# Two attention-and-MLP layers on one core: query ratio on GpSimd, parked sums joined by VectorE, a last step in open banks, and a new order

## The chip, the cores and the metric

The kernel runs on one core of one Trainium2 chip. The metric is device time in microseconds, from the first to the last instruction of an execution and a little around it; the time before is the median of three runs.

Five engines have queues of their own. TensorE (PE) multiplies, VectorE (DVE), ScalarE (ACT) and GpSimd (POOL) do elementwise work, and SyncE (SP) issues all data transfers. Results of PE land in eight PSUM banks of 512 float32 columns each.

## The reference

```python
def _A_ref(x, wqkv, w_phi, wo):          # S = 2048 rows, D = 512, H = 32 heads of 16
    q, k, v = split(x @ wqkv)
    pq, pk = q @ w_phi, k @ w_phi        # per head
    phi_q = concat([softmax(pq), softmax(-pq)])
    phi_k = concat([softmax(pk), softmax(-pk)])
    kv = einsum("bhsf,bhsd->bhfd", phi_k, v)     # sums over all rows
    z  = einsum("bhsf->bhf", phi_k)
    num = einsum("bhqf,bhfd->bhqd", phi_q, kv)
    den = einsum("bhqf,bhf->bhq", phi_q, z)[..., None] + 1e-6
    return (num / den) @ wo

def _B_ref(x, w1, w2):                   # hidden width 1792
    return maximum(x @ w1, 0) @ w2

x = x + _A_ref(layernorm(x), ...)
x = x + _B_ref(layernorm(x), ...)
x = x + _A_ref(layernorm(x), ...)        # the same weights once more
x = x + _B_ref(layernorm(x), ...)
```

## The kernel before

Each float32 product is made of three float16 products (high by high, high by low, low by high: `PAIRS`). The 2048 rows are 16 chunks of 128 (`NCH`), and two chunks make one of the eight tiles of the MLP (`NT`).

**A layer.** Every chunk is normalised (`front_norm`), its keys and values are projected (`keys`, `values`), and `gather` adds the products of key features and values to the running sums. The sums of 16 pairs of heads are spread over three groups (`SPANS`: 7, 7 and 2 pairs, 66 columns each). When all 16 chunks are in, `summary` folds the two 33-column halves of each pair together and makes the right-hand side of the numerators. Each chunk's query goes through `query` and `look`; `numerators`, `turn` and `back_project` finish the attention; then come the MLP's tiles in seven steps each (`tile_steps`).

**Products by seven.** Most MLP tiles compute a 2x2 block product with seven products instead of eight. `hidden_by_seven` issues those of the first weight in one PSUM bank `ph`: ACT saves parts of the bank (`snap`, L1484), DVE adds a saved part in the middle of each step (`plus`, L1490) and two at its end (`both`, L1495), and PE goes on after those. `out_by_seven` does the same for the second weight, in four banks (y0, y1, kv1, kv0) that stay open over the steps of a tile; `leave` takes the four banks out into the two row blocks `xa` and `xb` with ACT, DVE and POOL. The last step of the last tile is computed plainly: `mlp_out` for the first chunk and `last_rows`, in two halves, for the second, in banks of their own, each with its own DVE addition to the rows (L1602, L1622).

**Parked sums.** In layer 0's last tiles the next layer's sums are gathered already, while the banks kv0 and kv1 are wanted by `out_by_seven`. So after chunk 9 ACT copies the sums aside (`save`, L896), chunks 10 and 11 are made in another bank and added by DVE (`added`, L887), and at chunk 12 the sums are put back into banks by multiplying them with the identity on PE (`back`, L873).

**The query features.** `feature_map` with `psum=False` computes, per chunk, two softmaxes over 16 columns: DVE takes the sums and the ratio of the two (`ratios`, L728 to L730), ACT raises one half and makes a guard (L734, L738), POOL multiplies the other half by the ratio (`product`, L747), ACT rounds (L757), POOL makes the low part (L761), and SP turns the result into `pT`.

**The order.** Each task of the kernel names its engine, its reads and its writes; the task's number beside it is the planner's estimate of its duration. `ORDER` holds one long string per engine, in which each character says which of the tasks still left on that engine comes next. The five queues are thus written out by hand; waits between engines follow from the reads and writes.

Of the kernel before, what the change touches and what calls it, by code (L numbers as in the profile page):

```python
# [9 lines left out]
F32 = mybir.dt.float32  # L10
# [8 lines left out]
P = 128  # L19
# [6 lines left out]
LAG = 2  # L26
# [6 lines left out]
ASIDE = 2 * (NT - 3)  # L33
# [25 lines left out]
        "000033220100220031000010000a190840055051391301538473008402a0302920a302100105206020612031F051C4B20z133140"  # L59
        "3140304770663gg00ee10cccc0bbbb0iaagafae00170605500302011900110000010045030004061110001215020033040045000"  # L60
        "78008809a00101156360541022110600020000000600700000000000000000000050700d00bh000j000000g00000000000000000"
        "0011111333333330222444444133022233344440022222222000000000111220000033007c000000080000000002000002200000"
        "0000000201111100000200300000000000000070900f000c0hm000000j000j0000000000e0000000000000011111111111333333"
        "33302233341330222222222222222233344444440355044445555566677788888aaa099900770600446666660044400222222222"
        "22011111100000000000000000001111110110000111000011111444440302222255555555044444488077777066605999999999"
        "9990880020000050090000090000000000000001111111110010p0oq012l0l1jj000hgg000fddddi00b10dff0ccccc00aaa09900"
        "770004444407383366304031105005040000022010001105504444555aaaaaaaaaaaaaaaaaaabbbccccccccdddeee00200999000"
        "6620033330222011111111100500600000000h00i00000000000f00000000l0000L00000J0000000V0000000000O00000R000000"
        "000000000000000000H00000000000000X00000000000000000J000000000000000000000000E00F00000000000C000000000000"
        "000000000000000p000000000000000000000000000000p00000000000h00000000s000s0000000000000000000h000000000000"  # L70
        "0i0L000L0000000000U00000000000000000000D000000000000000000000q0000000000u0000000000000000000000000000000"
        "00000000000000000000000000000000000000000000000000000000000000000000000000000000000000000000000000000000"
        "000000000000000000000000000000000000000000000000000000000000000010",
    DVE:
        "330343302321000f51441192412111601c0b33j0503584c730g2230c000e0YYd0g00eS044e4Ndg66Jie0500440a302h20f1h11f0"
        "0g00i0d7063c5b55c04a44033300111441026051002m32k2k3j22g22222b2233232282335i2340e2d211116191lt127i52n2fl30"
        "0112018f12d9940002660779bb0891aa0781c0b1520362001bb141070013131152131216310361756715073056050a402001411c"
        "3b222843120123350242000011111133443022504030a0181062e2d0101900001313115213121150416886716910706625000801"
        "601000111136306216552407363343514030999g0ff002d201091000006320314047312161241103001025223003602401060500"
        "8001650067555402844002201066014007732200h4g0001221180000005704003010000000373024010000000k01i00h0f0000b0"  # L80
        "a01001b1a403700030g20e10cx2w01511101030tl232p255mMM24090HO0N70Zd7Zc76I0Z8285804123a491201Z2Z201ZxZ06Zvb1"
        "01j30Zoi3042Zt10Zr21h11fZl000ZOZO112cc01100ZE1190m1315j013101101k1ZtZtj0231005232200220Zc062521072252102"
        "2e2002b21020200243228800220770b25o21062501h0220022102hh3060042320b0290170a292800221020102010202005223200"
        "2200201020102000220023000233201022002210221020000010011010",
    ACT:
        "00424312110044010002005cbbb5a02me9kd808260dm310j2902dl2kc1040uZq30kk3213mmZhZg02Zep722m5sll20o306ll62113"
        "61l2k4L212420kk421011023g01e1400301cc0131gg21131gg21131050102d3k42046212c12108lll80b0hh6c9e090f478664080"
        "2050bb009014d1039111c1054483203029i909006c14bee0a004688a000b20b90a8001669013404340605c505413674034534303"
        "62240063001c1600033101410041201206811645b444441320510133001556000434001103734305223228230042472104b41483"
        "025530222223601102024088b21009480b30010001211217460565042232721055a59088848477c01ab0ade0eii0d10e2420f008"  # L90
        "00668071905775533a39933393577303a23820732102016670085102403214130011400442008188b33101004100103730322204"
        "05040064301100050440j301g11821304016004090d8c80b0aa6a07500c4602202103030241310d03889a008058506n066l55i60"
        "60e5o8347kl06I0Hh90F840B6P76Zq6M687K7ZjI66Zh7b070043Z8Zo440ZY220Zi4Zi4r41Zd33ZL440ZJ0010ZVs33ZB3024442ZK"
        "2ZZm24ZI401114102200302200504x23015400228100Z75247163ZA00Zzm120041033204002Zi01Zw10220105040302404312Zc1"
        "16052406024420006410322501L307250130200502330s60130262005j04416304427030604e0204102200302620143022614002"
        "620055040605203005104032500302500302040022003020103022040302000303201030220002221400221030200000",
    POOL:
        "10002540850058006800960A70y8016810960060908a000790070a1180900700020106252201b010837b205500550010e10c0i0h"
        "00bj0i09b18d0c700d52035103009080560500020550700570104523221111403000113020100304443300112313101100101112"
        "1504009240353403212111400002013101114104443301034300010010bb0a010777090555556601433302002011022201110000"  # L100
        "0050030000000030010000011100330000066605000000000a091000200b009cc0kk0uY29s0U8110Z00110Vj1Zm20Zk11m0Zp003"
        "302222g201Zc111ZB1111000070n01100100201121330211d11040310111T1411Y152202113302203302141101008222u2225000"
        "0504131102d2201330211d1211122017000070010330005222002221100044403333333333331000000000022201110000000000",
    SP:
        "30200110102600169d30520bx6c47c40rce6g16545d03401x9331dy1ac2111007k24h20g1123q131001b606gld02f20u2is03231"
        "34273Af5732de22eb11ec141441a99n129524b139339383b7982769b749488a66214g0307b36375a2df567426e3a90826i554007"
        "36272pb76777468694a947k7264f4284748c2f2g21e3410a121d14992308d82bb7ba275100447036502702n2ma419773745t1t31"
        "23p160p5t06061000E3030z12a02630h720pd010rl1170uaa60B097e20h3B0a1Jdd20Nbe5Vjbcea0baj2T484p7Z04ea44q98d038"
        "252552P130200i04053607240441b2260511706329203201191505036026424330015511551441302203022200010",
# [173 lines left out]
def tile_kernel(ctx: ExitStack, tc: tile.TileContext, x_in, wqkv, w_phi, wo, w1, w2, out):  # L283
# [17 lines left out]
            "rhs0": 1, "rhs1": 1, "r46": 2, "s46": 5, "s46a": 4, "yT": 2, "oT": 2, "h0": LAG + 3, "h1": LAG + 3, "w2": 3, "sn": 2}  # L301
# [360 lines left out]
    def feature_map(src, inv, up, side, psum, fast, name, pool=fr, tags=("e", "p16")):  # L662
# [17 lines left out]
        for h in range(0, H, n):  # L680
# [45 lines left out]
            def ratios(of=piece_of):  # L726
                sm, e3 = of()[2], of()[5]
                nc.vector.tensor_reduce(sm, e3, axis=AX.X, op=ALU.add)  # L728
                nc.vector.reciprocal(sm[:, H:], sm[:, H:])
                nc.vector.scalar_tensor_tensor(sm[:, H:], sm[:, :H], HALF, sm[:, H:], op0=ALU.mult, op1=ALU.mult)  # L730
# [128 lines left out]
    def gather(l, c):  # L859
# [6 lines left out]
        parted, again = ASIDE <= c < ASIDE + CPT, c == ASIDE + CPT  # L866
        if c == 0 or again:
            kv_bank[l] = [bank(f"kv{i}", f"kv{i}_{l}_{c}") for i in range(2)]
        if again:
            def back():  # L870
                for i, (b, a) in enumerate(zip(kv_bank[l], aside)):
                    b.ap = b.make()
                    nc.tensor.matmul(of_pairs(b.ap, i), ident, of_pairs(a.ap, i), start=True, stop=False,  # L873
                                     skip_group_check=True)

            add(PE, 1.56, back, reads=aside, makes=kv_bank[l])
        if not parted:
            sums_of_pairs(l, c, range(2), kv_bank[l], c == 0, c in (NCH - 1, ASIDE - 1))
        for i in range(3) if parted else (2,):
            b, a = bank("n", f"kvn{i}_{c}"), rest if i == 2 else aside[i]  # L880
            sums_of_pairs(l, c, [i], {i: b}, True, True)

# [1242 lines left out]
```

## Time and profile before

| what | value |
|---|---|
| median of three runs | 963.53 us |
| lowest of them | 962.7 us |
| profiled execution | 964.9 us |
| its span | 962.8 us |
| granted TensorE clock, mean | 0.999 |
| instructions | 23735 |

The profile is of one execution. Its page gives each engine's busy time, the span in 40 slices, the chain of work that ended last, the costliest groups of instructions, and the transfers. Other views group instructions by line, list who waited for whom, or show a stretch in order of time. PE is TensorE's products and PEld its weight loads, which overlap them; a "q" behind an engine's name is its sequencer, and SPq issues transfers. In a group's row stand the line, the engine, the operation, output<-input, the count, and behind the bar the busy time in us and the mean of one in ns. In a row of one line's view stand minimum, median and maximum in ns. In a timeline row stand start and duration in us, and in brackets the idle time before it with what ended it.

### The profile page before, as it was taken

How to read it: one execution, taken by the hardware profiler on the slowest of the kernel's cores; microseconds unless marked ns; L12 is line 12 of the kernel's file. 1: busy time of each engine (PE TensorE's matmuls, PEld its weight loads, DVE VectorE, ACT ScalarE, POOL GpSimd, SP SyncE). 2: the span in 40 equal slices, each digit the busy share in tenths (PEclk: the TensorE clock that was granted, in tenths of full speed). 3: DMA queues.
4: the chain of work that ended last, by engine and by line, in shares of the span. 5: the costliest groups of instructions: out<-in, count | busy, mean ns of one | idle time of the engine just before them, and what ended most of it. 6: DMA issues, size and time to landing. Idle time of an engine off the chain costs nothing.

```text
span 962.8 us, 23735 instructions
## 1 busy us (share of the span) xinstructions
PE 948.0 (98%) x9368; PEld 658.8 (68%) x9368; DVE 708.2 (74%) x1445; ACT 588.2 (61%) x1161; POOL 618.8 (64%) x634
## 2 busy tenths in 40 slices
PE   8999999999999999999999999999999999999997
PEld 6544455665665666667677875566666989888997
DVE  6999988876977778676476678887887566655554
ACT  8999888754564646455365555566556566555553
POOL 2697865758874757655277646256377887777563
PEclk9999999999999999999999999999999999999999
DMA  8657459469689696968739765579899776956441
GB/s 309 211 160 219 132 145 240 92 144 211 176 216 256 170 219 180 238 176 213 194 122 271 254 203 155 169 189 262 202 225 238 217 176 152 219 135 187 141 136 64
DMA packets 251839, 183.38 MB, mean 190 GB/s; under 512 B 180688, under 2 KB 188112, under 8 KB 251728
## 3 DMA queue, kind: packets, MB, share of 16 engines
q1 hardware_dynamic: 251728, 181.87, 72.1%
q8 instruction: 73, 1.20, 0.6%
q14 instruction: 38, 0.31, 0.1%
HBM read 108.30 MB, written 30.15 MB: 144 GB/s over the span
## 4 chain that ended last, share of the span: by engine, by line
PE 85%; DVE 5%; DMA 5%; ACT 2%; POOL 2%; issue 1%; SPq 0%; DVEq 0%; POOLq 0%; ACTq 0%
PE ph L1471 22%; PE py L1587 13%; PE py L1646 12%; PE pk L653 8%; PE pv L653 8%; PE pq L653 8%; PE pw L653 7%; PE ph L1551 3%; DMA oT<-n_o 2%; PE pn L1056 2%; PE kv L852 1%; DMA s<-s_dram 1%; DMA st_k<-in_A_wqkv_dram 1%; DVE fm_q L728 0%; POOL n_o L570 0%
## 5 line engine op out<-in xcount | busy, mean ns | idle before, releaser
L1587 PE MATMUL py<-w,h 128*128 128x512 f16 x690 | 174.5, 379 | 0.0
L1484 ACT ACTIVATE sn<-ph 128x128 f32<-128x128 f32 x294 | 80.7, 274 | 151.2 <-PE ph L1471 147.6
L1471 PEld LDWEIGHTS <-s 128*128 128x128 f16 x2352 | 151.2, 98 | 27.1 <-issue 3.1
L653 PEld LDWEIGHTS <-xT 128*128 128x128 f16 x900 | 86.8, 98 | 98.2 <-issue 1.7
L1471 PEld LDWEIGHTS <-w 128*128 128x128 f16 x1764 | 111.0, 98 | 13.8 <-DVE h L1202 0.6
L1471 PE MATMUL ph<-yT,s 128*128 128x128 f16 x1176 | 97.6, 219 | 2.5 <-DVE ph L1490 2.4
L1471 PE MATMUL ph<-yT,w 128*128 128x128 f16 x1176 | 97.6, 219 | 0.0
L1587 PEld LDWEIGHTS <-h 128*128 128x128 f16 x690 | 61.3, 98 | 47.4
L1490 DVE TENSOR_TENSOR ph<-ph,sn 128x128 f32<-128x128 f32 x98 | 29.3, 299 | 87.0 <-PE ph L1471 50.3
L761 POOL TENSOR_TENSOR p_q<-e_q,p_q 128x1024 f16<-128x1024 f32 x32 | 72.3, 2260 | 24.8 <-ACT p_q L757 24.7
L653 PE MATMUL pw<-wo_h,oT 128*128 128x512 f16 x256 | 81.2, 379 | 2.1 <-DMA oT<-n_o 1.9
L750 POOL TENSOR_TENSOR e_k<-e_k,fm_k 128x1024 f32<-128x1024 f32 x30 | 58.4, 1948 | 36.3 <-ACT fm_k L742 31.1
L653 PE MATMUL pv<-wv_h,xT 128*128 128x512 f16 x256 | 81.5, 379 | 0.0
L653 PE MATMUL pk<-wk_h,xT 128*128 128x512 f16 x256 | 81.5, 379 | 0.0
L761 POOL TENSOR_TENSOR p_k<-e_k,p_k 128x1024 f16<-128x1024 f32 x30 | 67.2, 2241 | 21.7 <-ACT p_k L757 19.8
L653 PEld LDWEIGHTS <-oT 128*128 128x128 f16 x384 | 36.7, 98 | 44.4 <-DMA oT<-n_o 4.1
L1646 PEld LDWEIGHTS <-h 128*128 128x128 f16 x648 | 59.2, 98 | 7.3 <-issue 0.7
L1495 DVE TENSOR_TENSOR ph<-ph,sn 128x256 f32<-128x256 f32 x98 | 41.9, 427 | 28.7 <-PE ph L1471 27.8
L747 POOL TENSOR_TENSOR e_q<-e_q,fm_q 128x512 f32<-128x512 f32 x32 | 33.9, 1060 | 41.2 <-DVE dn L1064 17.7
L1267 POOL TENSOR_TENSOR w<-r 128x256 f32<-128x256 f32 x41 | 32.7, 797 | 40.5 <-ACT r L1263 37.1
L653 PE MATMUL pq<-wq_h,xq 128*128 128x512 f16 x168 | 56.8, 379 | 0.3 <-ACT qs L922 0.2
L1646 PE MATMUL py<-w,h 128*128 128x256 f16 x324 | 53.0, 272 | 0.4 <-POOL w L1267 0.3
(282 smaller groups left out, 2455.0 us busy)
## 6 DMA issues: line engine op xcount, KB each, us to landing
s<-s_dram SPq DMA_DIRECT2D x98, 512.0 KB, 4.4
q_dram<-qs SPq DMA_DIRECT2D x28, 256.0 KB, 2.9
ql<-q_dram SPq DMA_DIRECT2D x28, 256.0 KB, 3.5
u<-t_dram SPq DMA_DIRECT2D x13, 512.0 KB, 4.8
xt_dram<-xT SPq DMA_DIRECT2D x21, 256.0 KB, 4.0
xq<-xt_dram SPq DMA_DIRECT2D x21, 256.0 KB, 4.1
xe<-in_A_x_dram SPq DMA_DIRECT2D x16, 256.0 KB, 4.1
x<-in_A_x_dram SPq DMA_DIRECT2D x16, 256.0 KB, 4.0
```

The lines of the kernel that those rows point to most:

```text
L653: nc.tensor.matmul(pm.ap, xT.ap[:, a, k, :], W.ap[b][:, k, :], start=(k == 0 and i == 0), stop=(k == KC - 1 and i == 2))
L747: nc.gpsimd.tensor_tensor(e3[:, H:], e3[:, H:], sm[:, H:].unsqueeze(2).to_broadcast([P, H, DH]), op=ALU.mult)
L750: (nc.vector if fast else nc.gpsimd).tensor_tensor(e3, e3, sm.unsqueeze(2).to_broadcast([P, 2 * n, DH]), op=ALU.mult)
L761: (nc.vector if fast else nc.gpsimd).tensor_sub(part16(1, cols), part16(1, cols, ef), part16(0, cols))
L1267: nc.gpsimd.tensor_sub(rf.ap[:, :2, :], r.ap.rearrange("p (a b) -> p a b", a=4)[:, ::3, :], block(1).unsqueeze(1).to_broadcast([P, 2, P]))
L1471: nc.tensor.matmul(at(r), weight_of(i, b, kk, s, summed), rows_of(y, i, a, kk), start=(first and kk == 0 and n == 0), stop=(kk == 1 and n ...
L1484: nc.scalar.activation(saved(i), at(2), AF.Copy)
L1490: add(DVE, 0.27, lambda: nc.vector.tensor_tensor(at(3), at(1), saved(2), op=ALU.add), reads=[(ph, 1), (sn, 2)], writes=[(ph, 3)], boost=10 ...
L1495: add(DVE, 0.40, lambda: nc.vector.tensor_tensor(wide(ph), wide(ph), wide(sn), op=ALU.add), reads=[(sn, 0), (sn, 1)], writes=[(ph, 0), (ph ...
L1551: nc.tensor.matmul(at()[:, j, cs.start * P:cs.stop * P], W1.at(b, k, slice(f * P, (f + 1) * P)), yT.ap[:, cs, a, k, :], stop=(k == KC - 1 ...
L1587: nc.tensor.matmul(py.ap, h[a].ap.rearrange("p j t -> p (j t)")[:, cols], W2.at(b, fs[j], slice(0, D)), start=(begins and j == k == 0), st ...
L1646: nc.tensor.matmul(py.ap[:, 256 * r:256 * r + 256], left[a], right[b], start=(s == 0 and r == 0 and k == 0), stop=(last and k == 2), skip_ ...
```

## The change

1. **Query ratio.** DVE keeps the sums and the reciprocal. ACT scales the reciprocal (`level`), POOL multiplies it by the other sums (`ratio`) ahead of its product.
2. **Parked sums.** The sums set aside are kept with their two halves already folded: one ACT copy of 33 columns per pair and one DVE addition. Chunks 10 and 11 are added in two pieces per group. `back` is gone: chunk 12 starts its banks fresh, and `summary` adds the parked sums on DVE. They lie in columns of the first weight's buffer that held one of four early folds, so these have three places.
3. **Last step.** The plain step of the last tile accumulates in banks that the seven products left open (the first chunk's in the fourth bank, the first half of the second chunk's in the third), and `leave` takes both out at once. The other half keeps a bank of its own.
4. **Order.** All five strings are new. (They differ nearly from the first character on and are left out here.)

```diff
-ASIDE = 2 * (NT - 3)
+ASIDE = CPT * (SECOND[0].start - 1)
+AGAIN = NCH - 2 * CPT
...
-"s46a": 4
+"s46a": 3
...
-                nc.vector.scalar_tensor_tensor(sm[:, H:], sm[:, :H], HALF, sm[:, H:], op0=ALU.mult, op1=ALU.mult)
+            def level(of=piece_of):
+                sm = of()[2]
+                nc.scalar.activation(sm[:, H:], sm[:, H:], AF.Copy, scale=HALF)
+            def ratio(of=piece_of):
+                sm = of()[2]
+                nc.gpsimd.tensor_tensor(sm[:, H:], sm[:, H:], sm[:, :H], op=ALU.mult)
...
-                add(DVE, 1.62, ratios, reads=[(e, h)], writes=[(fm, h)])
+                add(DVE, 1.53, ratios, reads=[(e, h)], writes=[(fm, h)])
+                add(ACT, 0.162, level, reads=[(fm, h)], writes=[(fm, "-")])
...
-                add(POOL, 1.0, product, reads=[(fm, h)], writes=[(e, "-")])
+                add(POOL, 0.31, ratio, reads=[(fm, h)], writes=[(fm, "-")])
+                add(POOL, 1.02, product, reads=[(fm, "-")], writes=[(e, "-")])
...
-        parted, again = ASIDE <= c < ASIDE + CPT, c == ASIDE + CPT
+        parted, again = ASIDE <= c < AGAIN, c == AGAIN
...
-        if again:
-            def back():
-                for i, (b, a) in enumerate(zip(kv_bank[l], aside)):
-                    b.ap = b.make()
-                    nc.tensor.matmul(of_pairs(b.ap, i), ident, of_pairs(a.ap, i), start=True, stop=False, ...)
-            add(PE, 1.56, back, reads=aside, makes=kv_bank[l])
         if not parted:
-            sums_of_pairs(l, c, range(2), kv_bank[l], c == 0, c in (NCH - 1, ASIDE - 1))
+            sums_of_pairs(l, c, range(2), kv_bank[l], c == 0 or again, c in (NCH - 1, ASIDE - 1))
...
+            if i < 2:
+                for j in range(2):
+                    add(DVE, ..., partial(plus_half_of, a.ap, a.ap, b, i, j), reads=[b], writes=[a])
+                continue
...
-                aside.append(f32_tile("b", f"kva{i}"))
-                def save(b=b, a=aside[-1], i=i):
-                    a.ap = a.make()
-                    nc.scalar.activation(of_pairs(a.ap, i), of_pairs(b.ap, i), AF.Copy)
-                add(ACT, 0.46, save, reads=[b], makes=[aside[-1]])
+                aside.append(a := Res())
+                a.ap = W1.part(0, i).rearrange("p (a b) -> p a b", a=2)[:, 1, 3 * P:].bitcast(F32)[:, :33 * 7] ...
+                add(ACT, 0.29, lambda a=a, b=b, i=i: nc.scalar.activation(a.ap, of_pairs(b.ap, i)[:, :, :33], AF.Copy), ...)
+                add(DVE, 0.33, partial(plus_half_of, a.ap, a.ap, b, i, 1), reads=[b], writes=[a])
+    def plus_half_of(o, x, b, i, j):
+        nc.vector.tensor_tensor(o, of_pairs(b.ap, i)[:, :, 33 * j:33 * j + 33], x, op=ALU.add)
...
+            if l == 1 and i < 2:                       # in summary
+                for j in range(2):
+                    def joined(i=i, b=b, j=j):
+                        ...
+                        plus_half_of(o, o if j else aside[i].ap, b, i, j)
+                    add(DVE, 0.33, joined, reads=[b, aside[i]], ...)
+                continue
...
-        begins = s == 0 or alone                       # in mlp_out
-        if (l, c, s) == (1, NCH - 1, NP - 1):
+        final = (l, t, s) == (1, NT - 1, NP - 1)
+        begins = (s == 0 or alone) and not final
+        if final and i == 1:
             return last_rows(h, fs, rows[l, c])
+        if final:
+            outs[i] = outs[3]
...
+            if final:
+                leave(l, t, 3)
+            else:
-            add(DVE, 0.66, ...)
+                add(DVE, 0.66, ...)
...
-            py, cols = bank("nh"[r], f"py_last_{r}"), ...       # in last_rows
+            py, cols = bank("n", "py_last") if r else outs[2], ...
...
+            if not r:
+                leave(1, NT - 1, 2)
+            else:
-            add(DVE, 0.395, ...)
+                add(DVE, 0.395, ...)
...
+        waits = l == 1 and t == NT - 1 and n > 1       # in out_by_seven
-        if last:
+        if last and not waits:
             leave(l, t, n)
```

More of the change, by code (lines that the diff above doesn't have):

```diff
@@ L64 @@
[L64 to L68, printed above, removed]
@@ L940, in summary @@
         for i, b in enumerate(banks):
+            if l == 1 and i < 2:
+                for j in range(2):
+                    def joined(i=i, b=b, j=j):
+                        if i == j == 0:
+                            whole.ap = whole.make()
+                        o = of_all()[:, SPANS[i].start:SPANS[i].stop]
+                        plus_half_of(o, o if j else aside[i].ap, b, i, j)
+                    add(DVE, 0.33, joined, reads=[b, aside[i]], makes=[(whole, i)] if i == j == 0 else [],
+                        writes=[] if i == j == 0 else [(whole, i)])
+                continue
             def joined(i=i, b=b):
@@ L1226, in home_of_early_folds @@
         s = plan.buf("s46a", lambda name=f"fs_{n}": [f16(0), f16(1)])
-        return r, s, [], plain["w1"] if k < 4 else []
+        return r, s, [], plain["w1"] if k < 3 else []
     early_folds = [0]
@@ L1247, in home_of_folds @@
         s = plan.buf("s46", lambda name=f"fs_{n}": [f16(0), f16(1)])
-        ends = [t for b in plan.lines["s46a"][-4:] for t, _, _ in b.uses]
+        ends = [t for b in plan.lines["s46a"][-3:] for t, _, _ in b.uses]
         return r, s, plain["w2"] if k < 2 else [], ends if k < 4 else plain["w2"] if k == 4 else []
@@ L1610, in last_rows, with go @@
         for r in range(2):
-            py, cols = bank("nh"[r], f"py_last_{r}"), slice(r * D // 2, (r + 1) * D // 2)
-            def go(py=py, cols=cols):
-                py.ap = py.make()
+            py, cols = bank("n", "py_last") if r else outs[2], slice(r * D // 2, (r + 1) * D // 2)
+            def go(py=py, cols=cols, r=r):
+                if r:
+                    py.ap = py.make()
                 for j in range(2):
@@ L1618, in go @@
                                          h[a].ap.rearrange("p j t -> p (j t)")[:, (2 * j + 1) * P:(2 * j + 2) * P],
-                                         W2.at(b, fs[j], cols), start=(j == k == 0), stop=(j == 1 and k == 2))
-            add(PE, 0.66, go, reads=[*h, *dict.fromkeys(W2.res[f // 2] for f in fs)], makes=[py])
-            add(DVE, 0.395, lambda py=py, cols=cols: nc.vector.scalar_tensor_tensor(
+                                         W2.at(b, fs[j], cols), start=(r == 1 and j == k == 0),
+                                         stop=(j == 1 and k == 2), skip_group_check=not r)
+            add(PE, 0.66, go, reads=[*h, *dict.fromkeys(W2.res[f // 2] for f in fs)], makes=[py] if r else [],
+                writes=[] if r else [py])
+            if not r:
+                leave(1, NT - 1, 2)
+            else:
+                add(DVE, 0.395, lambda py=py, cols=cols: nc.vector.scalar_tensor_tensor(
                 x.ap[:, cols], py.ap[:, cols], S_["inv_2"].ap, x.ap[:, cols], op0=ALU.mult, op1=ALU.add),
@@ L1646, in go @@
                     nc.tensor.matmul(py.ap[:, 256 * r:256 * r + 256], left[a], right[b],
-                                     start=(s == 0 and r == 0 and k == 0), stop=(last and k == 2),
+                                     start=(s == 0 and r == 0 and k == 0), stop=(last and k == 2 and not waits),
                                      skip_group_check=True)
```

113 lines of the change are left out of this document (63 added, 50 removed).

## The prediction

> **What bounds the kernel now.** I read the page first: busy times, the slices, and the shares of the chain that ended last.
>
> ```profile
> PE 948.0 (98%) x9368; PEld 658.8 (68%) x9368; DVE 708.2 (74%) x1445; ACT 588.2 (61%) x1161; POOL 618.8 (64%) x634
> PE   8999999999999999999999999999999999999997
> PE 85%; DVE 5%; DMA 5%; ACT 2%; POOL 2%; issue 1%; SPq 0%; DVEq 0%; POOLq 0%; ACTq 0%
> ```
>
> TensorE (PE) is busy 948.0 of 962.8 us and is 85% of the chain. Only two things can shorten this kernel: work taken out of PE's queue, and the 14.8 us in which PE does nothing. The other four engines have 250 us and more of idle time, so work moved among them counts only where PE ends up waiting. Next, busy time by stage, cut at the front, the change of layer and the tail. The columns are the stretch, its length, then busy time and count for PE, weight loads, DVE, ACT, POOL; then clock, DMA share and GB/s.
>
> ```profile
> 0.00:20.00 20.00, 16.63 (x106) 12.17 (x107) 12.94 (x42) 15.49 (x32) 5.55 (x21) 1.00 0.87 310
> 20.00:580.00 560.00, 555.59 (x4959) 352.83 (x4957) 432.44 (x844) 357.86 (x639) 370.81 (x332) 1.00 0.74 194
> 580.00:640.00 60.00, 59.78 (x454) 33.19 (x452) 53.06 (x117) 35.42 (x64) 28.79 (x24) 1.00 0.62 175
> 640.00:949.00 309.00, 307.13 (x3774) 253.49 (x3772) 202.23 (x431) 176.60 (x424) 209.84 (x254) 1.00 0.74 186
> 949.00:962.80 13.80, 8.88 (x83) 7.13 (x81) 7.49 (x14) 2.79 (x6) 3.77 (x6) 0.91 0.11 38
> ```
>
> Length minus the first busy column is PE's idle time: 3.4 us in the front, 4.4 + 0.2 + 1.9 = 6.5 us in the 929 us of the body, 4.9 us in the tail. The view of waits says who ends the body's idle time: total, times, longest.
>
> ```profile
> PE ph L1471 <- DVE ph L1490: 2.4, 4, 0.9
> PE pw L653 <- DMA oT<-n_o: 1.9, 3, 1.0
> ```
>
> So the body's waits are few, under about 1 us each, and belong to the order: a new order can remove them and make others.
>
> **The parked key-value sums.** The old code loads the parked sums back into PSUM by multiplying them with the identity on TensorE.
>
> ```profile
> 584.15 1.55 PE kv L873 x4
> L944 DVE TENSOR_REDUCE kvs<-kv x4: 627/633/639, 141.3 to 608.5; 128x231 f32<-128x462 f32 x4
> L887 DVE TENSOR_TENSOR kva<-kvn,kva x4: 626/628/629, 534.8 to 546.8; 128x462 f32<-128x462 f32 x4
> L896 ACT ACTIVATE kva<-kv x2: 550/554/557, 496.4 to 496.9; 128x462 f32<-128x462 f32 x2
> L1490 DVE TENSOR_TENSOR ph<-ph,sn x98: 284/300/300, 272.0 to 950.0; 128x128 f32<-128x128 f32 x98
> L1495 DVE TENSOR_TENSOR ph<-ph,sn x98: 406/431/433, 274.1 to 951.5; 128x256 f32<-128x256 f32 x98
> 607.94 1.19 DVE L944 TENSOR_REDUCE kvs<-kv 128x231 f32<-128x462 f32 x2
> 609.84 0.29 PE L955 MATMUL zsum<-kvs,both_halves 128*128 128x16 f32 x2
> ```
>
> The first row is a piece of the chain: four PE instructions, 1.55 us, with PE running before and after them. They go entirely: **-1.55 us**.
>
> In exchange DVE joins in pieces of 231 columns, from PSUM plus SBUF. The nearest rows of that kind are L1490 (128 columns, 300 ns) and L1495 (256 columns, 431 ns); on the line between them 231 columns take 0.40 us. Chunks 10 and 11: eight of these, 3.2 us, instead of four at 0.63, 2.5 us. The save at chunk 9: two ACT copies of 231 columns (below 0.55 us each) and two DVE pieces, 0.8 us. The summary: four pieces, 1.6 us, for two reductions whose joint row is 1.19 us, so 0.3 to 0.4 us later. That latency lies on the way to the stacked product (L955), which started 0.7 us after that row's end, behind query products that do not need it. I cost it at nothing; without those products on PE ahead of L955 it costs 0.4 us. The parked sums move to weight columns that served as a fold's fourth place, so three places remain. A step's fold is consumed three steps later, ahead of the write that now reuses its place; cost nothing, or one ACT wait of about half a microsecond.
>
> **The last step.** Timeline of the tail, old kernel: start, duration, engine, line.
>
> ```profile
> 955.57 1.46 PE L1587 MATMUL py<-w,h 128*128 128x512 f16 x6
> 955.79 2.77 POOL L1692 TENSOR_TENSOR x<-x,v 128x256 f32<-128x256 f32 x3 [5.57 <-DVE v L1678]
> 956.87 1.47 PE L1617 MATMUL py_last<-w,h 128*128 128x256 f16 x12
> 957.28 0.75 DVE L1725 SCALAR_TENSOR_TENSOR x<-py,inv,x 128x512 f32<-128x512 f32 x1
> 958.14 0.75 DVE L1602 SCALAR_TENSOR_TENSOR x<-py,inv,x 128x512 f32<-128x512 f32 x1
> 958.81 0.47 DVE L1725 SCALAR_TENSOR_TENSOR x<-py,inv,x 128x256 f32<-128x256 f32 x1
> 959.20 0.86 DVE L1622 SCALAR_TENSOR_TENSOR x<-py_last,inv,x 128x256 f32<-128x256 f32 x2
> 959.70 0.83 SPq L1625 DMA_DIRECT2D out_dram<-x  x2
> ```
>
> PE ends at 958.34; DVE goes on to 960.06; then the stores and the close take 2.7 us to 962.8. DVE works on PE's results in five pieces: 0.75 + 0.75 + 0.47 + 0.86 for two. With the last plain step added in the banks already open, L1602 and one of the two L1622 go. PE does the same 18 products. The two merged DVE pieces now wait for the plain products, not only for the seven-product groups: the 512-column one for those that end at 957.03, which is before its old start; behind it in DVE's queue is only the tail. What comes last next? The second half of xb needs POOL's three subtractions and sums, which end at 958.56, and PE's last product at 958.34. So the last DVE piece starts at about 958.7, not 959.59 (960.06 less 0.47): **-0.9 us**. Removing the two pieces alone would give 0.75 + 0.43 = 1.18; POOL takes the rest. L1692's longest took 1.10 instead of 0.73 us; one more such delay leaves a gain of 0.5.
>
> **The ratio of the query sums.** DVE's multiply of 32 columns (L730) becomes an ACT scaling and a POOL product.
>
> ```profile
> L730 DVE SCALAR_TENSOR_TENSOR fm_q<-fm_q x32: 191/256/1999, 55.9 to 793.7; 128x32 f32<-128x32 f32 x32
> L730 DVE SCALAR_TENSOR_TENSOR fm_q<-fm_q 128x32 f32<-128x32 f32 x32 | 15.3, 479 | 1.1
> 719.82 2.00 DVE fm_q L730
> 722.91 0.49 PE L1471 MATMUL ph<-yT,s 128*128 128x128 f16 x6 [0.86 <-DVE ph L1490]
> L738 ACT ACTIVATE eps_q<-fm_q x32: 212/221/236, 57.6 to 842.2; 128x32 f32<-128x32 f32 x32
> L633 POOL TENSOR_TENSOR stat_b<-stat_b,nhalf x32: 547/550/1576, 160.4 to 877.0; 128x1 f32<-128x1 f32 x32
> L1282 POOL TENSOR_TENSOR r<-r,w x41: 453/456/1317, 738.6 to 949.2; 128x128 f32<-128x128 f32 x41
> L1692 POOL TENSOR_TENSOR x<-x,v x6: 724/732/1103, 578.9 to 957.8; 128x256 f32<-128x256 f32 x6
> 617.44 0.19 DVE L730 SCALAR_TENSOR_TENSOR fm_q<-fm_q 128x32 f32<-128x32 f32 x1
> 617.78 1.06 POOL L747 TENSOR_TENSOR e_q<-e_q,fm_q 128x512 f32<-128x512 f32 x1 [13.46 <-DVE dn L1064]
>   DMA pT<-p_q: 0.5, 1
> ```
>
> DVE loses 32 x 0.479 = 15.3 us. The undisturbed instruction is 0.19 us, so 9.2 us of that were held up; the longest, 2.00 us at 719.82, sits on the chain and is followed by a PE wait of 0.86 us. ACT gains 32 x 0.22 = 7 us (L738 has that size). No row has a POOL product of 32 columns: 128 columns take 456 ns, 256 take 732, and the line through them gives 0.25; a one-column power takes 0.55. I take 0.30, nearer the line: 10 us for POOL, 8 to 18 at the ends. A hop from DVE to POOL is 617.78 - 617.63 = 0.15 us. Per query the chain becomes 0.15 + 0.22 + 0.15 + 0.30 = 0.82 instead of 0.48 + 0.15 = 0.63 us, or 0.34 undisturbed: 0.2 to 0.5 us later. Queued behind the new ACT scaling are the raised half and the guard, 0.2 us later too. What hides it: PE waited once, 0.5 us, for a transposed query tile (last row). With that cover gone each late query costs up to 0.5 us. Relief is worth up to the 0.86 us, and the new order may have made it moot: **-0.3 us**, with -0.9 and 0 as ends.
>
> The Trainium skill (GPSIMD Engine Reference, Engine selection) speaks against this part: it sends elementwise work to VectorE and calls GpSimd about 2x slower on two inputs. The rows agree on the direction, 0.25 to 0.55 against 0.19 us; by the rule alone the part would be a loss. The Trainium skill (SBUF — State Buffer, Who interferes with whom) says that a DVE instruction with two SBUF inputs and a GpSimd one exclude each other for a whole instruction, which fits the 191 to 1999 ns of L730 and would have the new GpSimd products hold up DVE elsewhere.
>
> **The order.** All five queues are rewritten. It adds no PE work. Nothing in the trace prices it beforehand, so I take 0 with ends from the body's idle time: -3.3 if half of the 6.5 us goes, +5 if three quarters as much again comes.
>
> **Sum.** The profiled execution took 964.9 us (span 962.8 and 2.1 around it). 964.9 - 1.55 - 0.9 - 0.3 = 962.15. It lies 1.37 us above the median of the runs shown, 963.53; carried over, **960.8 us**.
>
> **Rivals.**
> - *More waits on DVE's middle sum* (slower side). In each of 98 steps PE needs L1490 in the middle; 4 waits now cost 2.4 us, 0.6 each. If the new order leaves longer DVE pieces ahead of it, five more such waits eat the 2.75 us, and ten more give 960.8 + 6 = 966.8. For it: DVE is 77% busy in 20 to 580, the merging adds 231-column pieces there, and the old order shows what one held-up piece does. Against it: DVE also loses 15.3 us. It decides from the fifth added wait on.
> - *The identity product's time is not returned*: PE waits at the opening of layer 1 instead, because a latency chain sets that stage. Against it: only 0.2 us idle in 580 to 640. 962.4.
> - *The order closes half of the body's waits*: 960.8 - 3.3 = 957.5. For it: the longest waits are ones that an order can move.
> - *Queries come late*, through the longer path over POOL: 32 x 0.5 = 16, so 977. Against it: one wait of 0.5 us in the old trace. The Trainium skill (GPSIMD Engine Reference, Engine selection) is the rule on that side.
> - That the tail returns 0.5 and not 0.9, because POOL stays the last, lies inside the forecast.
>
> **How the numbers follow.** Forecast (959 to 963.5) 0.50; more DVE waits (964 to 968) 0.22; time not returned 0.12; half of the waits closed 0.12; late queries 0.04. The range reaches from just below the third rival to the first with eleven waits (960.8 + 6.6): 957.0 to 967.5, leaving out the late queries and the far ends of the order. Two per cent, about what a measurement of this kernel can tell from no change, is 19 us; PE's removed work and all of its idle time in the body together are 8 us. Faster by over 2%: 0.01; within: 0.97; slower by over 2%: 0.02, half of the late queries.
>
> **What would show it.** PE busy about 946.4, no L873 row; a last DVE piece that starts within 0.4 us of PE's end; a POOL product of 32 columns at 0.25 to 0.55 us; the body's PE idle time near 6.5 us. The prediction is wrong if that idle time is far from it, which is the order's doing, or if PE's instructions take other times.

## The result, and the profile after

The changed kernel takes 957.4 us, median of nine runs (955.23 to 960.62), against 963.53 before: ratio 0.9939, 95% interval [0.9922, 0.9956], or 6 us less. A second set of runs later gave 0.9937 [0.9914, 0.9959]. One run of the kernel before took 1321.21 us and is left out of the ratio. The forecast was 960.8 with a range of 957.0 to 967.5.

The profiled execution is the fastest of the nine (955.23 us), and that of before was slower than its median, so the traces lie 9.3 us apart (spans 962.8 and 953.5) where the medians lie 6.1 apart. Differences between these two traces as a whole are therefore larger than what the change is worth on the median.

The page of the changed kernel: busy times, PE's slices, shares of the chain that ended last.

```profile
PE 944.3 (99%) x9364; PEld 657.6 (69%) x9364; DVE 685.9 (72%) x1419; ACT 593.4 (62%) x1193; POOL 622.0 (65%) x666
PE   8999999999999999999999999999999999999998
PE 96%; ACT 1%; DMA 1%; DVE 0%; issue 0%; POOL 0%; POOLq 0%; SPq 0%; DVEq 0%
```

PE is now 96% of the chain instead of 85%. The 5% that DVE held has gone. DMA's 5% is down to 1% here, but in a second profiled execution of the same kernel, below, the chain is 93% PE and 4% DMA, so that part differs from one execution to the next. PE's busy time and idle time by stage, the same view and columns as in the prediction, cut at the same points of the work:

```profile
0.00:20.00 20.00, 16.96 (x108) 12.14 (x109) 13.53 (x44) 15.93 (x34) 5.56 (x21) 1.00 0.91 329
20.00:580.00 560.00, 558.25 (x4994) 355.16 (x4993) 423.90 (x841) 360.59 (x655) 376.44 (x351) 1.00 0.74 194
580.00:640.00 60.00, 59.97 (x497) 34.66 (x494) 52.09 (x114) 38.12 (x76) 28.36 (x26) 1.00 0.65 177
640.00:940.00 300.00, 299.45 (x3685) 247.75 (x3684) 189.72 (x411) 175.69 (x424) 207.30 (x263) 1.00 0.76 189
940.00:953.50 13.50, 9.69 (x94) 7.90 (x91) 6.67 (x13) 3.04 (x7) 4.35 (x6) 1.00 0.21 75
```

PE's idle time in the body is 1.75 + 0.03 + 0.55 = 2.3 us, where it was 6.5; 3.0 in the front (3.4); 3.8 in the tail (4.9). That is 5.6 us less waiting, of which 4.2 in the body. The rest of the 9.3 us is PE's busy time, 3.7 less, of which the identity product is 1.55. The two groups of waits that the prediction showed (total, times, longest) now read:

```profile
PE ph L1495 <- DVE ph L1514: 0.9, 2, 0.5
PE pw L656 <- DMA oT<-n_o: 0.2, 1, 0.2
```

They were 2.4 us for DVE's middle sum and 1.9 us for the turned rows. The tail, in the timeline (start, duration, engine, line):

```profile
947.60 2.79 POOL L1730 TENSOR_TENSOR x<-x,v 128x256 f32<-128x256 f32 x3 [5.56 <-DVE v L1716]
948.04 1.46 PE L1614 MATMUL py<-w,h 128*128 128x512 f16 x6
948.91 1.37 DVE L1763 SCALAR_TENSOR_TENSOR x<-py,inv,x 128x256 f32<-128x256 f32 x2
949.33 0.82 PE L1649 MATMUL py_last<-w,h 128*128 128x256 f16 x6
950.42 0.48 DVE L1659 SCALAR_TENSOR_TENSOR x<-py_last,inv,x 128x256 f32<-128x256 f32 x1
950.93 0.33 SPq L1662 DMA_DIRECT2D out_dram<-x  x1
```

PE ends at 950.15 and the span at 953.5: 3.35 us, before 962.8 - 958.34 = 4.46. The last DVE piece starts at 950.42, 0.27 after PE's end and right after POOL's third sum at 950.39. DVE does three pieces for PE's results instead of five.

The moved work, as groups of one line (duration min/median/max in ns, first and last start):

```profile
L740 POOL TENSOR_TENSOR fm_q<-fm_q x32: 247/253/872, 56.3 to 793.8; 128x32 f32<-128x32 f32 x32
L736 ACT ACTIVATE fm_q<-fm_q x32: 212/229/241, 55.8 to 786.1; 128x32 f32<-128x32 f32 x32
  ACT fm_q L736: 38.1, 14
L909 DVE TENSOR_TENSOR w<-kvn,w x8: 383/388/399, 530.4 to 538.4; 128x231 f32<-128x231 f32 x8
603.37 0.69 DVE L909 TENSOR_TENSOR kvs<-kv,kvs 128x231 f32<-128x231 f32 x2
605.09 0.29 PE L978 MATMUL zsum<-kvs,both_halves 128*128 128x16 f32 x2
```

The POOL product of 32 columns takes 253 ns and ACT's scaling 229; POOL sits idle for 38.1 us in all ahead of that product (third row), which no wait of PE above shows. The last join ends at 604.06 and the stacked product starts at 605.09, 1.03 us later with query products on PE between, so the longer join at the summary is still covered.

### The profile page after: what moved, and what is told of

Read it like the earlier page. It is cut to its first block, busy times and chain, and to the rows that moved or that the text cites. A ratio compares the mean times of both kernels' runs of the same rounds, so it can differ in the third digit from the quotient of the medians.

```text
span 953.5 us, 23741 instructions
## 1 busy us (share of the span) xinstructions
PE 944.3 (99%) x9364; PEld 657.6 (69%) x9364; DVE 685.9 (72%) x1419; ACT 593.4 (62%) x1193; POOL 622.0 (65%) x666
## 4 chain that ended last, share of the span: by engine, by line
PE 96%; ACT 1%; DMA 1%; DVE 0%; issue 0%; POOL 0%; POOLq 0%; SPq 0%; DVEq 0%
PE ph L1495 24%; PE py L1614 15%; PE py L1684 13%; PE pw L656 9%; PE pv L656 9%; PE pq L656 9%; PE pk L656 9%; PE ph L1575 4%; PE pn L1079 2%; PE kv L864 1%; DMA oT<-n_o 0%; DMA st_k<-in_A_wqkv_dram 0%; PE pv L843 0%; PE pf_q L1847 0%; PE tr_a L599 0%
## 5 line engine op out<-in xcount | busy, mean ns | idle before, releaser
L1495 PEld LDWEIGHTS <-w 128*128 128x128 f16 x1764 | 111.0, 98 | 13.2 <-DVE h L1225 0.6
L1225 DVE SCALAR_TENSOR_TENSOR h<-ph,h 128x512 f16<-128x512 f32 x58 | 39.3, 681 | 18.8 <-ACT h L1222 18.8
```

The source lines that it names most:

```text
L1225: add(DVE, 0.607, lambda: nc.vector.scalar_tensor_tensor(h[1].ap, at(), 0.0, h[0].ap, op0=ALU.max, op1=ALU.subtract), reads=[ph, h[0]], wr ...
L1495: nc.tensor.matmul(at(r), weight_of(i, b, kk, s, summed), rows_of(y, i, a, kk), start=(first and kk == 0 and n == 0), stop=(kk == 1 and n ...
```

## The experiments

All ratios are to the kernel before on the same chip. Between two ratios the difference is given with the root of the squared half-widths; the changed kernel is taken as 0.9938, the middle of its two sets, with 0.0014 on either side. A thousandth is about 1 us.

### Code and order apart

The new code in the old order and the old code in the new order. In each, the instructions common to both keep the other kernel's sequence; the few that differ were put by hand where their counterparts stand.

```diff
-        "0000222222110104100001100070088006600413318011593473108302a0302901a02211013517002060013GG00E1D4420133140"
...
+        "000033220100220031000010000a190840055051391301538473008402a0302920a302100105206020612031F051C4B20z133140"
...
```

> The changed code in the five old queues; only the tasks that are new (scaling on ScalarE, product on GpSimd, the joins in pieces) are put in where the old ones stood, and the last three results follow the new tail. Theory 'order': the new queues closed the body's waits, worth 3 to 4 us of the 6.1; then this keeps the old waits and comes to 963.5 - 1.55 - 0.9 - 0.3 = 960.8, PE's idle time in the body near 6.5 us. Theory 'relief': taking the small ratio off VectorE closed the waits; then this comes to about 957.4 with 3 us or less of idle time in the body.

Measured: 962.31 us, ratio 0.9978 [0.9966, 0.9991].

> The old code in the new queues; the identity product stands just ahead of the sums of chunk 12, the last results follow the old tail. Theory 'order': 957.4 + 1.55 + 1.0 + 0.3 = about 960.3, with the body's waits near those of the changed kernel. Theory 'relief': the new queues alone are worth nothing, 963 to 964.

Measured: 965.07 us, ratio 1.0012 [0.9999, 1.0025].

The first two rows are of the new code in the old order: its busy times, and its body summed over 20 to 940 (length, then busy time of each engine). The third is the same sum for the old code in the new order, and the fourth for the changed kernel.

```profile
PE 947.6 (99%) x9364; PEld 660.0 (69%) x9364; DVE 692.3 (72%) x1419; ACT 591.9 (62%) x1193; POOL 626.1 (65%) x666
sum 920.00, PE 913.97 PEld 632.18 DVE 671.09 ACT 570.97 POOL 613.81; mean PE 304.66 PEld 210.73 DVE 223.70 ACT 190.32 POOL 204.60
sum 920.00, PE 914.64 PEld 631.47 DVE 679.23 ACT 565.93 POOL 600.11; mean PE 304.88 PEld 210.49 DVE 226.41 ACT 188.64 POOL 200.04
sum 920.00, PE 917.67 PEld 637.57 DVE 665.71 ACT 574.40 POOL 612.10; mean PE 305.89 PEld 212.52 DVE 221.90 ACT 191.47 POOL 204.03
```

PE's idle time in the body: 6.0 us with the code alone, 5.4 with the order alone, 2.3 with both (3.8 in a second profiled execution, below). The code alone is worth 2.1 us (0.0022 ± 0.0013), about the three terms that the forecast summed to 2.75; the order alone is worth nothing or less. Given the new code, the new order is worth 0.0040 ± 0.0019, some 3.9 us. So neither of the two theories holds alone: 'relief' asked for 957.4 with the code alone, and 'order' asked for 960.3 with the order alone. Together the two halves give 0.0062, which is 0.0052 ± 0.0023 more than they add up to one by one. The hand-placed instructions are a caveat: a better place for them could make either half look better.

The first row has a second lesson. That kernel has no identity product either, and PE is busy 947.6 us, against 948.0 before. Over all the runs here whose PE has these 9364 instructions, its busy time lies between 944.3 and 948.0 us. A change of one or two us in that figure is therefore not by itself a sign of work taken out.

### One part undone at a time, in the new order

The ratio back on DVE, in all 32 query pieces:

```diff
+                nc.vector.scalar_tensor_tensor(sm[:, H:], sm[:, :H], HALF, sm[:, H:], op0=ALU.mult, op1=ALU.mult)
...
-                add(ACT, 0.162, level, reads=[(fm, h)], writes=[(fm, "-")])
...
-                add(POOL, 0.31, ratio, reads=[(fm, h)], writes=[(fm, "-")])
```

> The changed kernel with the ratio back on VectorE in one instruction, everything else as changed, same queues less the 64 small tasks. Theory 'order': 957.4 to 958, nearly no loss. Theory 'relief': 960 to 961, since the small instruction held up by GpSimd makes TensorE wait again; its longest rows are again 1 us and more.

Measured: 960.43 us, ratio 0.9962 [0.9946, 0.9978]: 0.0024 ± 0.0021 above the changed kernel, 2.3 us. From its trace, the group of the ratio, the body's sum, and four pieces of the chain that leads through the opening of layer 1:

```profile
L731 DVE SCALAR_TENSOR_TENSOR fm_q<-fm_q x32: 191/209/1504, 55.5 to 790.3; 128x32 f32<-128x32 f32 x32
sum 920.00, PE 915.63 PEld 633.78 DVE 680.48 ACT 566.93 POOL 601.32; mean PE 305.21 PEld 211.26 DVE 226.83 ACT 188.98 POOL 200.44
615.29 3.09 DVE e_q L706
633.12 0.75 DVE fm_q L731
633.87 0.61 DVE wk_h L1172
634.52 0.72 PE ph L1484 x10
```

DVE's body grows by 14.8 us. PE's idle time in it is 4.4 us, against 2.3 and 3.8 in the two executions of the changed kernel. Between 606 and 634 the chain is mostly DVE's, with 3.5 us of POOL, where in the changed kernel all its pieces in that stretch but 0.03 us are PE's. The third row is an instruction whose median is 1.22 us. The fourth is the ratio itself, at 0.75 instead of 0.19, right ahead of the low part of a turned tile (`wk_h`) that PE waits for. This is what theory 'relief' had asked for: 960 to 961, and longest rows of 1 us and more.

The parked sums put back by the identity product:

```diff
+                    nc.tensor.matmul(of_pairs(b.ap, i), ident, of_pairs(a.ap, i), start=True, stop=False,
+                                     skip_group_check=True)
...
+            add(PE, 1.56, back, reads=aside, makes=kv_bank[l])
...
-                    add(DVE, 0.33, joined, reads=[b, aside[i]], makes=[(whole, i)] if i == j == 0 else [],
```

> The changed kernel with the parked sums handled as before: parked whole, joined back by the identity product on TensorE just ahead of chunk 12's sums, the summary's reductions as before; queues as changed otherwise. Theory 'returned in full': TensorE's removed 1.55 us is worth 1.5 to 2, so 959 to 959.7 against 957.4. Theory 'swallowed by the opening of layer 1': within 0.5 of the changed kernel.

Measured: 960.1 us, ratio 0.9955 [0.9939, 0.9970]: 0.0017 ± 0.0021, 1.6 us. The product is on the chain again, PE before and after it:

```profile
577.79 1.94 PE pq L656 x9
579.73 1.55 PE kv L885 x4
581.28 0.44 PE kv L864 x14
```

The size is that of the row, but the interval includes no effect at all.

The last plain step in banks of its own:

```diff
-        begins = (s == 0 or alone) and not final
+        begins = s == 0 or alone
...
-            py, cols = bank("n", "py_last") if r else outs[2], slice(r * D // 2, (r + 1) * D // 2)
+            py, cols = bank("nh"[r], f"py_last_{r}"), slice(r * D // 2, (r + 1) * D // 2)
```

> The changed kernel with the last plain step in banks of its own again and the five old results on VectorE at the end. Both theories: the time from TensorE's last product to the end of the span goes from 3.4 back to about 4.4 us, so 957.4 + 1.0 = 958.4. If GpSimd is what ends the tail either way, less than 0.5.

Measured: 959.67 us, ratio 0.9946 [0.9925, 0.9968]: 0.0008, inside both intervals. Its tail:

```profile
950.80 1.47 PE L1641 MATMUL py_last<-w,h 128*128 128x256 f16 x12
953.13 0.87 DVE L1646 SCALAR_TENSOR_TENSOR x<-py_last,inv,x 128x256 f32<-128x256 f32 x2
```

PE ends at 952.27 and DVE at 954.00, 1.73 us later; in the changed kernel that is 950.90 - 950.15 = 0.75. The trace shows the 1 us in place; the times alone could not settle it. The three undone parts add to 0.0024 + 0.0017 + 0.0008 = 0.0049 of the 0.0062, each with an interval of 0.002 or more.

### Where the ratio costs

The ratio on DVE for the five query pieces at the opening of layer 1 only, and then for the 27 others only.

```diff
+        on_dve = not psum and name in ('q1_0', 'q1_1', 'q1_2', 'q1_3', 'q1_4')
...
+                if on_dve:
+                    nc.vector.scalar_tensor_tensor(sm[:, H:], sm[:, :H], HALF, sm[:, H:], op0=ALU.mult, op1=ALU.mult)
...
+                if not on_dve:
+                    add(POOL, 0.31, ratio, reads=[(fm, h)], writes=[(fm, "-")])
```

> The changed kernel unaltered, beside the next three. Every theory: 0.994 of the kernel before, 957 to 958.

Measured: 957.37 us, ratio 0.9937 [0.9914, 0.9959]. Its profiled execution has 920 - 916.23 = 3.8 us of idle time in the body, so the 2.3 above is one draw, and a difference of one or two us between single executions shows little:

```profile
sum 920.00, PE 916.23 PEld 635.68 DVE 664.65 ACT 572.50 POOL 610.36; mean PE 305.41 PEld 211.89 DVE 221.55 ACT 190.83 POOL 203.45
```

> The changed kernel with the ratio back on VectorE for 5 of the 32 query chunks alone, those whose features are made from 570 to 640 us around the change of layers (layer 1's chunks 0 to 4). Theory 'opening': the relief acts where VectorE is nearly full, so this loses most of the 2 us that all 32 lost: about 959.5, with TensorE waits of 1 us or so from 600 to 640. Theory 'everywhere': 5/32 of it, 0.3 us, about 957.8.

Measured: 958.38 us, ratio 0.9945 [0.9929, 0.9961].

> The other 27 query chunks have the ratio back on VectorE, the five around the change of layers keep the changed form. Theory 'opening': within 0.7 of the changed kernel, 957.4 to 958.1. Theory 'everywhere': 27/32 of the 2 us, about 959.2.

Measured: 959.96 us, ratio 0.9953 [0.9936, 0.9969].

The two add to 0.0007 + 0.0015 = 0.0022, near the 0.0024 of all 32. The middles speak for a loss that is spread and against the opening alone, where the chain row of 3.09 us pointed. But neither part is clear of its interval of 0.002, which is as large as the whole loss, so neither theory is excluded.

### Is it DVE's time, or what holds DVE up?

The changed kernel, untouched but for one more DVE instruction a query piece, whose result nothing uses: one SBUF input and 32 columns; two SBUF inputs and 32 columns, the old ratio's form; one input and 304 columns. Beside them the changed kernel without the ratio.

```diff
                 nc.vector.reciprocal(sm[:, H:], sm[:, H:])
+                nc.vector.tensor_reduce(fm.ap[:, :H], sm[:, :H].unsqueeze(2), axis=AX.X, op=ALU.max)
...
+                nc.vector.scalar_tensor_tensor(fm.ap[:, :H], sm[:, :H], HALF, sm[:, H:], op0=ALU.mult, op1=ALU.mult)
...
+                nc.vector.tensor_reduce(fm.ap[:, :19], e3[:, :19], axis=AX.X, op=ALU.max)
```

> Changed kernel in its own order, and in each of the 32 query pieces one more DVE instruction of 32 columns with a single SBUF input (a reduction over a length of one, result unused). No other engine waits for anything new but DVE's next instruction. It adds about 0.1 to 0.2 us of DVE time a piece, 3 to 6 us in all. 'Held up': DVE's instructions with two SBUF inputs are the ones that GpSimd's work delays, a one-input one is not; then this costs at most 0.5 us: 957.4 to 957.9, ratio 0.994. 'DVE time': any instruction ahead of the query sums' end makes the parts late; about +2 us as with the ratio back on DVE: 959.5, ratio 0.996. 'Order only': DVE has slack, the time doesn't change: 957.4.

Measured: 957.86 us, ratio 0.9933 [0.9915, 0.9950].

> Changed kernel in its own order, and in each of the 32 query pieces one more DVE instruction of 32 columns with two SBUF inputs (the old ratio's form and place on DVE, its result unused). ACT's scaling and POOL's product stay. 'Held up': the longest take 1 to 2 us instead of 0.19, and it costs about what the ratio on DVE cost, +2 us: 959.5, ratio 0.996, while the one-input instruction costs at most 0.5. 'DVE time': +2 us in both. 'Chain': the ratio on DVE cost time since GpSimd's product had to wait for DVE; here the product does not hang on it more than on DVE's queue, and the time stays at 957.4, ratio 0.994.

Measured: 961.12 us, ratio 0.9970 [0.9958, 0.9981].

> Changed kernel in its own order with one more DVE instruction a query piece, with one SBUF input again, but of 304 columns, so that it takes about the mean time that the two-input one took with its delays (435 ns, 13.9 us for 32 pieces; an estimate from 128 ns for 32 and 676 ns for 512 columns of the same operation). 'DVE time': what the two-input instruction cost came from its mean duration, wherever it comes from; then this costs the same, 960.5 to 961, ratio 0.997. 'Delays': the same time in even pieces of 0.43 us is taken by DVE's slack, and the cost comes from the few pieces of up to 1.5 us, or from what they hold up; then 957.4 to 958.3, ratio 0.993 to 0.9945.

Measured: 959.73 us, ratio 0.9955 [0.9939, 0.9971].

> Changed kernel in its own order without the ratio: ACT's scaling, GpSimd's product of 32 columns and the DVE instruction are all left out (the query sums' ratio is not formed, GpSimd's large product uses the plain reciprocal). 32 scalings of 0.22 us and 32 products of 0.25 us go, 7.2 us of ACT and 8.1 us of POOL. 'Moved off DVE for nothing': what the change put on ACT and POOL is hidden, the time stays at 957.4, ratio 0.994. 'New place costs too': ACT's and POOL's part of the ratio costs PE time in the body, then it is faster by what it costs, up to 1.5 us: 956, ratio 0.992.

Measured: 958.74 us, ratio 0.9950 [0.9935, 0.9966].

The added group and the body's sum, first of the one-input kernel, then of the two-input one, then of the long one-input one:

```profile
L733 DVE TENSOR_REDUCE fm_q<-fm_q x32: 127/128/130, 58.1 to 788.9; 128x32 f32<-128x32 f32 x32
sum 920.00, PE 917.60 PEld 636.45 DVE 669.92 ACT 575.76 POOL 610.73; mean PE 305.87 PEld 212.15 DVE 223.31 ACT 191.92 POOL 203.58
```

```profile
L733 DVE SCALAR_TENSOR_TENSOR fm_q<-fm_q x32: 191/193/1528, 55.7 to 791.7; 128x32 f32<-128x32 f32 x32
L733 DVE SCALAR_TENSOR_TENSOR fm_q<-fm_q 128x32 f32<-128x32 f32 x32 | 13.9, 435 | 1.1
sum 920.00, PE 914.23 PEld 632.52 DVE 680.95 ACT 571.70 POOL 610.07; mean PE 304.74 PEld 210.84 DVE 226.98 ACT 190.57 POOL 203.36
```

```profile
L733 DVE TENSOR_REDUCE fm_q<-e_q x32: 410/411/414, 57.8 to 790.7; 128x19 f32<-128x304 f32 x32
sum 920.00, PE 916.75 PEld 635.22 DVE 677.40 ACT 575.04 POOL 611.22; mean PE 305.58 PEld 211.74 DVE 225.80 ACT 191.68 POOL 203.74
```

The same place, the same queue, the same 32 columns: with one input every instance takes 127 to 130 ns, 4.1 us in all (32 x 128), and the time does not rise. With two inputs they take 191 to 1528 ns, 13.9 us in all, and the kernel loses 0.0037 ± 0.0021 against the one-input one, 3.6 us; PE's idle time in the body is 5.8 against 2.4 us.

What holds the two-input instruction up can be seen beside it. The same query piece in the timelines of the two kernels (start, duration, engine, line), first with two inputs, then with one, and a group of the two-input kernel:

```profile
156.00 2.12 POOL L772 TENSOR_TENSOR p_q<-e_q,p_q 128x1024 f16<-128x1024 f32 x1
156.65 1.53 DVE L733 SCALAR_TENSOR_TENSOR fm_q<-fm_q 128x32 f32<-128x32 f32 x1
158.21 0.23 ACT L737 ACTIVATE fm_q<-fm_q 128x32 f32<-128x32 f32 x1 [2.19 <-DVE fm_q L733]
158.21 2.15 POOL L772 TENSOR_TENSOR p_q<-e_q,p_q 128x1024 f16<-128x1024 f32 x1
158.56 0.13 DVE L733 TENSOR_REDUCE fm_q<-fm_q 128x32 f32<-128x32 f32 x1
L1088 DVE SCALAR_TENSOR_TENSOR dn<-pn,eps_q x64: 157/166/176, 149.4 to 855.7; 128x16 f32<-128x16 f32 x64
```

The two-input instruction starts inside a POOL instruction and ends at 158.18, just after that one's end at 158.12. All 14 instances above 200 ns have a POOL instruction running beside them. The one-input instruction starts inside the same POOL instruction and takes its usual 0.13 us. The two differ in their operation too, but the last row has the operation of the slow one with one input in PSUM, and its 64 instances are even.

How the held-up instruction costs PE time stays open, for the third row shows a second effect. ACT's scaling overwrites what the added instruction reads, so it waits for it: in all 32 pieces it starts after the added instruction's end. The query's way on to POOL is late as well as DVE's queue. So it was with the ratio on DVE, and this kernel does not tell the two apart. PE does not wait longer for DVE's middle sum, which is 0.9 us, twice, as in the changed kernel. The longest of its added waits in the body are for others:

```profile
PE ph L1496 <- DVE ph L1515: 0.9, 2, 0.5
PE tr_b L599 <- ACT xn_b L633: 1.0, 1, 1.0
PE pq L656 <- DMA xq<-xt_dram: 1.0, 1, 1.0
PE ph L1496 <- DMA s<-s_dram: 0.9, 1, 0.9
```

The long one-input kernel was to show what a slower DVE costs by itself: 32 x 411 ns = 13.2 us in even pieces cost 0.0017 ± 0.0021 against the changed kernel, 1.7 us, between the other two. Its interval reaches both neighbours, so it does not decide. It is not a pure counterpart either, since its added instruction reads other columns: in 15 of the 32 pieces ACT's scaling starts before that instruction has ended. Its trace does not show a cost of DVE. The first query product starts at 37.3 us in it and at 34.7 in the changed kernel, ahead of the first added instruction at 57.8. From there to the end of the span are 920.9 us, against 918.8 and 921.0 in the two executions of the changed kernel, 919.3 with the short one-input instruction and 924.1 with the two-input one. These are single executions.

Without the ratio 8 us of POOL and 7 us of ACT go, and the time does not fall (0.0012 ± 0.0021 above the changed kernel). What the change put on those two engines is hidden, to within 0.9 us. This kernel also warns against single traces: with nothing added to DVE, its profiled execution has 920 - 914.20 = 5.8 us of idle time in the body, as much as the two-input one.

## Why the prediction was right, and where it was not

The range and the sign held, and the bound of 2% was never near. But the range held by 0.4 us only, four of the nine runs lie below its lower end, and the band of 959 to 963.5, which had 0.50, was missed. The middle was 3.4 us too high. The time came out at the third rival's 957.5, which had 0.12, and that is in part luck: the rival has the order close waits by itself, and the order alone closed nothing that the time shows. By the prediction's own sign, an idle time in the body far from 6.5 us, its account of the order was wrong.

- **Identity product, -1.55.** No such row is left. Putting it back cost 1.6 us, with an interval of 2 us around it, so the term stands as a size and is not proved by the times. The rival that its time is not returned is not excluded either, only less likely. The estimate of 0.40 us for a 231-column join was right (388 ns), and so was the cover of the join at the summary. PE's busy time was put at 946.4 and is 944.3, in the second execution 944.9. Where the further 1.5 to 2 us come from is open: the 947.6 of the old order would fit a link with the waits, but the long one-input kernel has 948.0 with 3.3 us of idle time in the body.
- **Tail, -0.9.** The trace gives 1.1, with POOL setting the last piece as reasoned and a start 0.27 us after PE's end, inside the 0.4.
- **Ratio, -0.3, ends -0.9 and 0.** The sizes were right: 253 ns on POOL, near the line's 0.25, and 229 ns on ACT for 0.22. The value was not, though barely clear of its interval: 2.3 us by undoing it (± 2.0). The step that failed priced the relief by the one held-up instance that was followed by a PE wait, 0.86 us. But 9.2 us of delays were spread over DVE's queue. That a held-up two-input instruction costs time in the new order is shown by the added copy, 3.6 ± 2.0 us more than the one-input one. That it does so by many small shifts in an order with little slack is argued, not shown.
- **Order, 0, ends -3.3 and +5.** Given the new code it is worth 3.9 ± 1.8 us; with the old code 1.2 us on the other side, hardly different from nothing. The step took code and order as two terms to be added, and they are not. What in the code the new order needs stays open. DVE is 22.3 us less busy with both (708.2 to 685.9), but that does not decide alone: with only the ratio undone it is busy 702.1 us and most of the gain stays, while with the old code in the new order it is 703.8 and none does. The body's idle time, which I said would stay near 6.5 us, is 2.3 and 3.8 in the two executions.
- **Rivals.** *More waits on DVE's middle sum* did not come: 4 became 2, with the new code in the old order too. *Queries late through POOL* did not come: PE has no wait for a turned tile of query features (`pT`) in the changed kernel's trace, and leaving that path out gained nothing. By the Trainium skill (GPSIMD Engine Reference, Engine selection) moving this product to GpSimd would lose; the row is slower there, 253 against 191 ns undisturbed, and the kernel is faster with it there. Here the measurement decides. The Trainium skill (SBUF — State Buffer, Who interferes with whom) has a VectorE instruction with two SBUF inputs contend with a GpSimd one that reads SBUF. The trace agrees: 191 to 1528 ns, the long ones beside POOL, against 127 to 130 for one input.

## What to carry to other kernels

Price a small instruction by the mean it has in the trace, not by its shortest: 191 against 479 ns, 32 times over, hid a part that was forecast at 0.3 us and cost 2.3 ± 2.0 to undo. When a change frees a queue and rewrites its order, the two are one term: run each alone before you credit either. An engine with 25% of idle time can still hold up what a tight order needs, so look for spread in the durations of its smallest instructions. And when you add an instruction to test an engine's slack, see in the trace who waits for it: a copy whose result nothing uses can still stand in another engine's way.

## What was not expected of the hardware

A DVE instruction of 32 columns with two SBUF inputs varies eightfold with what POOL runs beside it (191 to 1528 ns), where one with a single input varies by 3 ns. GpSimd's product of the same 32 columns is hardly slower than DVE's at its best, 253 against 191 ns, and was 872 at worst. And PE's recorded busy time varied by 3.7 us (944.3 to 948.0) over the kernels with 9364 instructions on it.
